# An attention and MLP kernel: dummy matmuls in the front's gaps, measured TensorE durations in the build-time order, and two value tiles loaded earlier

## The chip, the core and the metric

The kernel runs on one core of one Trainium2 chip. The metric is the device time of one execution in microseconds (us). It is compared between kernels run in alternation on the same chip. "Same" means within 2%.

The readings are of the hardware profiler's trace. In its lines PE is the TensorE matmul, PEld the weight load, DVE VectorE, ACT ScalarE, POOL GpSimd and SP SyncE. Ends of matmuls are modelled there (one of 512 columns is given 379 ns, though the next starts 216 ns after it), so a PE that is busy all the time is not necessarily at its peak.

## The reference, cut to what matters

```python
# B, H, S, Nb, D = 8, 8, 576, 16, 64; d_model 512, d_ff 2048, 4608 tokens
k_all = np.concatenate([beacon_k, k], axis=2)
v_all = np.concatenate([beacon_v, v], axis=2)
scores = 1/sqrt(D) * q @ k_all.transpose(...)        # causal on the 576 tokens
a = softmax(scores)
x = (a @ v_all) in the shape [B*S, H*D]
h = x @ w_in
out = (max(h, 0) ** 2) @ w_out
```

A batch has four pairs of heads. The MLP works in nine chunks of 512 tokens. Its first stage multiplies by w_in, its second by w_out. Chunk 0 is made of tokens of batch 0 alone, so it can't start before batch 0's attention.

## The kernel before

The kernel has no loops in its program. At build time it makes a list of operations, each with an engine, an estimated duration, a priority and dependencies, and plays them through an event simulation of its own. What comes out is a fixed order of instructions for each engine. On the chip TensorE works through its instructions in that order and stands where an input isn't there. So the estimated durations are never executed; they only decide who stands before whom.

```python
class Order:
    def run(self):
        ...
            for e in engines:
                if free[e] > now + 1e-9:
                    continue
                best = ...            # the ready op of least prio, whose buffers are free
                if best is None:
                    best = fallback
                if best is None:
                    continue          # this engine idles, in the order's own time
                ...
                end = now + dur
                free[e] = end
                issued.append((op, e, now))
                ...
                # users on PE see it `late` us later than other engines do
                heapq.heappush(events, (seen + op.late, seq, "done_pe", op))
        ...
        for op, e, _ in issued:
            op.insts = op.emit(e)
```

Two of the operations, and the order of the first loads on the GpSimd queue (t0, t1 make a mask; p1k is k of pair 1 of batch 0; v0 the first 128 rows of batch 0's v; w0 a quarter of w_in):

```python
qk = add(f"qk{p}.{n}.{i}", "PE", 0.24 + cols / 2400.0, emit_qk, ...)
tp = add(f"tp{b}.{part}.{pr}{xs}", "PE", 0.1 + (0.1 if b == 0 else 0.075) * ns * len(xs), emit_tp, ...)

RANK = [(0, 0), (0, 1), (1, 0), (1, 1), (2, 0), (3, 0), (2, 1), (3, 1)]   # (pair, phase) of batch 0
SOFT = "t0 p1k p1q t1 p2k p2q p3k p3q v0 v1 v2 v3 v4 w0 w1 w2 w3".split()
```

Behind these loads come batch 1's k and q, batch 1's v, and w_out in quarters. The loads of the queue are issued one after another: in the timeline of the kernel before k and q of pair 1 at 2.39 and 3.15 us, of pair 2 at 4.36 and 5.05, of pair 3 at 5.67 and 6.29.

The softmax here doesn't subtract the row's maximum and nothing guards it: scores larger than these inputs give would overflow.

## Time and profile before

| | before |
|---|---|
| time, median of 3 executions | 344.12 us (343.36 to 344.19) |
| TensorE busy | 332.1 of 342.1 us |
| TensorE waiting, in all | 5.8 us, of which 4.3 at the very start |
| first matmul; first matmul with w_in | 4.31 us; 23.99 us |
| DMA share of the 16 engines from 5 to 35 us | 1.10 to 1.30 |

The table of waits of the kernel before, for TensorE; the columns are who waited for whom, us in total, times, longest:

```profile
PE ps L462 <- DVE qk_area L307: 4.9, 2, 4.3
PE strip L609 <- DMA kT<-qk_area: 0.4, 1, 0.4
PE ps L661 <- DVE vb L307: 0.3, 1, 0.3
PE ps L792 <- DVE qT L307: 0.2, 1, 0.2
```

After its first matmul TensorE waits for 1.5 us in all. But the same work is slow in the front. From the timeline of the kernel before (start us, us, engine, line, operation, operands, count): 12 transposes of batch 0 and 24 of batch 1, then 24 attention-value matmuls before and after 22 us.

```profile
8.14 0.69 PE L465 MATMUL ps<-ident,qk_area 96*64 96x96 bf16 x12
30.07 0.70 PE L465 MATMUL ps<-ident,qk_area 96*64 96x96 bf16 x24
...
18.44 1.50 PE L661 MATMUL ps<-vb,pt 128*128 128x65 bf16 x24
24.40 0.89 PE L661 MATMUL ps<-vb,pt 128*128 128x65 bf16 x24
```

Twenty-four transposes at 30 us take what 12 take at 8 us, and the same 24 matmuls shrink from 1.50 to 0.89 us (the last 0.06 to 0.15 us of each overlap the group behind it, since ends are modelled). In the chain of work the 24 matmuls take 1.44 us at 18.51 and 0.73 us at 24.57: I read that as TensorE at half clock, then at full clock. The page's clock row hides it:

```profile
PE   4999999999999999999999999999999999999995
PEclk9999999999999999999999999999999999999999
```

The trace's own record of the granted clock begins with the grant of full clock at 22.5 us, counted from the first instruction. What lies before that first record is shown as full (1.00 from 5 to 20 us, where the durations are doubled). From its first matmul to that grant TensorE was busy for 17.0 of 18.2 us. Below, the clock's "release" is the time from which the record gives full clock.

### The profile page before, as it was taken

The numbers are of one execution on the slowest core, as the hardware profiler recorded it, in microseconds if no ns is written. First come the engines' busy times: TensorE is split into PE (matmuls) and PEld (weight loads), VectorE is DVE, ScalarE is ACT, GpSimd is POOL, SyncE is SP. The second block draws the span as 40 slices with busy tenths as digits, with TensorE's granted clock in tenths as the row PEclk, the third lists the DMA queues.
The fourth block names the chain that finished last, engine by engine and source line by source line (L and its number), as shares of the span: only waits on it lengthen the run. The fifth ranks groups of instructions, "written<-read, shape, count | busy, mean of one in ns | idle before, by whom it ended". The sixth has DMA issues, their size and how long they took to land.

```text
span 342.1 us, 7180 instructions
## 1 busy us (share of the span) xinstructions
PE 332.1 (97%) x2886; PEld 176.4 (52%) x2886; DVE 169.4 (50%) x371; ACT 191.9 (56%) x287; POOL 92.5 (27%) x144
## 2 busy tenths in 40 slices
PE   4999999999999999999999999999999999999995
PEld 2578775444544544445458845444444544444442
DVE  6878975147437863277436643664246502301300
ACT  4776864387766753675347744675557226515611
POOL 9774803324415605041521053014000000000000
PEclk9999999999999999999999999999999999999999
DMA  8999979999999999699989997977210131011002
GB/s 147 210 207 218 206 124 215 209 241 210 193 192 251 245 187 200 145 219 212 208 136 235 158 216 145 229 159 134 86 63 2 24 107 63 0 61 64 0 31 92
DMA packets 143663, 51.68 MB, mean 151 GB/s; under 512 B 130670, under 2 KB 138382, under 8 KB 143630
## 3 DMA queue, kind: packets, MB, share of 16 engines
q1 hardware_dynamic: 135231, 42.25, 62.1%
q0 software_dynamic: 7904, 8.69, 14.8%
q8 instruction: 22, 0.36, 0.5%
q10 hardware_dynamic: 495, 0.30, 0.3%
q14 instruction: 11, 0.09, 0.1%
HBM read 37.22 MB, written 9.44 MB: 136 GB/s over the span
## 4 chain that ended last, share of the span: by engine, by line
PE 85%; DMA 8%; POOL 3%; DVE 2%; ACT 0%; issue 0%; SPq 0%; POOLq 0%; ACTq 0%
PE ps L792 34%; PE ps L827 34%; PE ps L661 8%; PE strip L609 7%; DMA stg<-in_v_dram 3%; DMA kT<-qk_area 2%; DMA stg<-in_q_dram 2%; DMA stg<-in_k_dram 1%; POOL qk_area L430 1%; PE ps L729 1%; POOL qk_area L307 1%; DVE qT L307 1%; DVE g L817 0%; PE ps L465 0%; POOL tri L291 0%
## 5 line engine op out<-in xcount | busy, mean ns | idle before, releaser
L827 PE MATMUL ps<-w_out,g 128*128 128x512 bf16 x576 | 133.8, 379 | 0.0
L792 PE MATMUL ps<-xT,w_in 128*128 128x512 bf16 (+3 forms) x704 | 133.4, 341 | 0.2 <-DVE qT L307 0.2
L624 ACT ACTIVATE pt<-strip 128x832 bf16<-128x832 f32 (+4 forms) x128 | 104.3, 863 | 39.9 <-PE strip L609 39.7
L792 PEld LDWEIGHTS <-w_in 128*128 128x128 bf16 x704 | 65.7, 98 | 56.4 <-issue 4.3
L808 ACT ACTIVATE g<-ps 128x512 bf16<-128x512 f32 (+2 forms) x119 | 67.0, 563 | 41.6 <-PE ps L792 40.9
L827 PEld LDWEIGHTS <-g 128*128 128x128 bf16 x576 | 52.7, 98 | 60.9 <-issue 3.2
L817 DVE TENSOR_TENSOR g<-g 128x1024 bf16<-128x1024 bf16 (+2 forms) x80 | 52.5, 659 | 61.8 <-ACT g L808 59.5
L307 POOL CAST qk_area<-stg 128x512 bf16<-128x512 f32 (+2 forms) x60 | 40.3, 679 | 73.5 <-DMA stg<-in_k_dram 58.8
L305 ACT COPY osb<-ps 128x512 f32<-128x512 f32 x28 | 16.4, 585 | 57.4 <-PE ps L827 51.3
L661 PEld LDWEIGHTS <-pt 128*128 128x128 bf16 (+1 forms) x960 | 37.8, 100 | 14.8 <-issue 3.5
L307 POOL CAST vb<-stg 128x512 bf16<-128x512 f32 (+1 forms) x39 | 26.1, 678 | 62.7 <-DMA stg<-in_v_dram 44.3
L661 PE MATMUL ps<-vb,pt 128*128 128x65 bf16 (+1 forms) x960 | 41.5, 197 | 0.3 <-DVE vb L307 0.3
L609 PE MATMUL strip<-qT,kT 64*128 64x80 bf16 (+6 forms) x400 | 37.3, 292 | 0.4 <-DMA kT<-qk_area 0.4
L681 DVE TENSOR_TENSOR xn<-ps,rcp 128x320 bf16<-128x320 f32 (+2 forms) x64 | 31.5, 492 | 2.3
L635 DVE TENSOR_TENSOR pt<-pt,tri 128x1024 bf16<-128x1024 bf16 (+1 forms) x36 | 23.7, 658 | 15.8 <-ACT pt L624 15.8
L810 DVE TENSOR_SCALAR g<-ps 128x512 bf16<-128x512 f32 (+2 forms) x41 | 24.4, 603 | 14.0 <-PE ps L792 13.5
L679 DVE RECIPROCAL rcp<-ps 128x5 f32<-128x5 f32 (+2 forms) x64 | 12.2, 191 | 34.9 <-PE ps L661 34.7
L609 PEld LDWEIGHTS <-kT 64*128 64x128 bf16 x400 | 12.4, 96 | 17.6 <-issue 12.6
L307 DVE COPY osb<-ps 128x512 f32<-128x512 f32 x8 | 5.5, 692 | 19.1 <-PE ps L827 19.0
L638 DVE TENSOR_TENSOR pt<-pt,tri 80x160 bf16<-80x160 bf16 x32 | 10.3, 320 | 0.0
L352 POOL DMA_DIRECT2D stg<-in_v_dram x10 | 8.5, 850 | 5.0 <-DMA w_in<-in_moe_w_in_dram 3.6
L307 DVE COPY kT<-ps 128x576 bf16<-128x576 bf16 (+3 forms) x11 | 6.5, 594 | 1.9 <-PE ps L465 1.0
(38 smaller groups left out, 64.6 us busy)
## 6 DMA issues: line engine op xcount, KB each, us to landing
out_dram<-osb SPq DMA_DIRECT2D x17, 512.0 KB, 3.9
stg<-in_q_dram SPq DMA_DIRECT2D x24, 256.0 KB, 5.5
stg<-in_k_dram SPq DMA_DIRECT2D x18, 256.0 KB, 5.1
stg<-in_v_dram SPq DMA_DIRECT2D x18, 256.0 KB, 4.6
w_in<-in_moe_w_in_dram POOLq DMA_DIRECT2D x4, 512.0 KB, 8.9
w_out<-in_moe_w_out_dram POOLq DMA_DIRECT2D x4, 512.0 KB, 11.3
stg<-in_v_dram POOLq DMA_DIRECT2D x6, 256.0 KB, 8.3
stg<-in_k_dram SPq DMA_DIRECT2D x6, 224.0 KB, 4.7
```

The costliest lines, as they stand in the source:

```text
L305: nc.scalar.copy(dst, src)
L307: eng[e].tensor_copy(dst, src)
L609: nc.tensor.matmul(st[:, hj, at:at + t1 - t0], kT[b % 2][hp, pr, 128 * c:128 * c + 128], qT[b % 2][hp, pr, t0:t1], start=True, stop=True,)
L624: nc.scalar.activation(pt[take_pt.held[2]][:, :, off:off + width], st[:, :, 0:width], AF.Exp, bias=0.0, scale=scale)
L635: nc.vector.tensor_tensor(out=d, in0=d, in1=tri[:, m0:m0 + m, :][:, None].to_broadcast([128, 2, m, 128]), op=ALU.min)
L661: nc.tensor.matmul(a[:, at + (t - tl[0]) * (D + 1):at + (t - tl[0] + 1) * (D + 1)], P[0:rr, hj, o:o + 128], vb[b % 2][0:rr, c, 2 * pr + hj ...
L681: nc.vector.tensor_tensor(out=xn[b % 2].rearrange("p t (h d) -> p h t d", d=D)[:, h0:h0 + nh, tl[0]:tl[0] + nt], in0=a[:, :, :, 0:D], in1= ...
L792: nc.tensor.matmul(h[:, lo - spans[0][0]:hi - spans[0][0]], w_in_sb[:, mc, ft * 128:(ft + 1) * 128], xT[:, mc, lo % RING:lo % RING + hi - lo],
L808: nc.scalar.activation(dst, h, AF.Relu, bias=0.0, scale=1.0)
L810: nc.vector.tensor_scalar(out=dst, in0=h, scalar1=0.0, scalar2=None, op0=ALU.max)
L817: nc.vector.tensor_tensor(out=d, in0=d, in1=d, op=ALU.mult)
L827: nc.tensor.matmul(o, G[:, fc, ts * 128:(ts + 1) * 128], w_out_sb[:, fc, :], start=(fc == 0), stop=(fc == NFT - 1))
```

## The change

Its intent: get TensorE's clock up early with dummy matmuls, keep it up by putting dummies wherever the order expects TensorE to idle until 22 us, correct the order's TensorE durations to those measured, load v0 and v1 ahead of batch 0's last pair, and hold back the TensorE users of some loads in the order.

```diff
+    FILL_UNTIL = 22.0
 ...
                     if best is None:
+                        if e == "PE" and 0.3 < now < self.FILL_UNTIL and self.pools["ps"]:
+                            cols = 128 if now < 4.0 else 256
+                            free[e] = now + 0.107
+                            issued.append((Op("fill", "PE", 0.107, lambda e, cols=cols, bank=self.pools["ps"][0]: self.fill(bank, cols)), e, now))
 ...
+    def emit_fill(bank, cols):
+        nc.tensor.matmul(ps[bank][:, 0:cols], g[1][:, 0, 0:128], g[1][:, 0, 0:cols], start=True, stop=True)
+    nc.vector.memset(g[1][:, 0, 0:256], 0.0)
 ... (cast of v: batch 0's users on TensorE 1 us later; first q and k casts 0.3, pair loads 0.5)
-                    tp = add(..., "PE", 0.1 + (0.1 if b == 0 else 0.075) * ns * len(xs), emit_tp,
+                    tp = add(..., "PE", 0.05 + (0.055 if b == 0 else 0.047) * ns * len(xs), emit_tp,
-            qk = add(f"qk{p}.{n}.{i}", "PE", 0.24 + cols / 2400.0, emit_qk,
+            qk = add(f"qk{p}.{n}.{i}", "PE", 0.2 + cols / 2400.0, emit_qk,
 ... (three more durations of this kind)
-    RANK = [(0, 0), (0, 1), (1, 0), (1, 1), (2, 0), (3, 0), (2, 1), (3, 1)]
+    RANK = [(0, 0), (0, 1), (1, 0), (2, 0), (1, 1), (3, 0), (2, 1), (3, 1)]
-    SOFT = "t0 p1k p1q t1 p2k p2q p3k p3q v0 v1 v2 v3 v4 w0 w1 w2 w3".split()
+    SOFT = "t0 p1k p1q t1 p2k p2q v0 v1 p3k p3q v2 v3 v4 w0 w1 w2 w3".split()
```

## The prediction

> **What bounds the kernel now.** From about 25 us on TensorE does: the table of busy time by stretch has it busy 10.00 of 10 us in nearly every stretch from 40 to 335 us, and the table of waits gives it 0.7 us of waiting there at most (0.4 us at 98 us, for the kT transpose DMA). So useful TensorE work moved earlier shortens the run, while ready work lasts. The page shows idle time only at the front: until 4.31 us, 0.58 us at 5.9, 0.34 us at 14.8.

> **What the change does.** (1) Dummy 128-column matmuls from about 1 us (estimate: 25 to 35, 107 ns each) and 256-column ones in the order's gaps until 22. I expect the full clock at 5 to 8 us, seen in halved durations. The 17 us of half-clock front are some 8.5 us of work at full clock. Cost: tenths of a us where a dummy precedes ready work. (2) v0 and v1 are issued before pair 3's k and q: about 1.3 us earlier (two issues of 0.63), landing before 14.1 us; that removes the v wait. Pair 3 lands later, but nine exps of 0.86 us precede it in the new ranking. (3) Shorter model durations reorder the program; total work stays.

> **How much survives.** ScalarE: batch 0 has 16 exps of 0.86 us, 13.8 us, now 7.1 to about 25 us with gaps; could end near 21. VectorE is busy 9.2 of 10 us at 30 to 40. The DMA engines are saturated (share over 1.1) from 5 to 35 us, so w_in's quarters still land at about 20.4, 22.9, 25.4 and 28 us (from waits on them), and the last first-stage matmuls of chunk 0 can't end before about 30; w_out lands at 44 to 49 us, and second-stage matmuls now begin at 47.7. So by 34 us the new kernel can be ahead by about 40 matmuls of 272 columns at 113 ns, 4.5 us; of it some is lost to a thinner stock before w_out lands and to VectorE. Estimate: 4.3 us saved, carried to the end because the late stretches are TensorE-bound with MLP work in stock.

> **Prediction:** 339.8 us, range 336.8 to 342.8; faster by over 2%: 0.14, within 2%: 0.83, slower by over 2%: 0.03.

> **What would show it.** Right: 96-column transposes near 27 ns each from about 8 us; last exp of batch 0 ending at about 21 us; first w_in matmul at about 21 instead of 24.0 us, the last 272-column one 4 us earlier; no new waits over 1 us after 50 us. Wrong: durations still doubled at 15 us; TensorE waiting for w_in, w_out or batch 1's k and q between 22 and 50 us by as much as was gained; the 98 us wait for kT grown to several us.

> **What would make it wrong.** The dummies don't release the clock, or it falls back; the reordering starves TensorE later; or w_in and w_out arrive earlier (then 335 to 337 us).

A front of 17 us taken for 8.5 us of work, less what the loads and VectorE hold back, a lead of 4.5 us by 34 us, of which 4.3 us saved; 344.1 less 4.3 is 339.8 us. The sum takes the full clock at 5 to 8 us for granted; the kernel before, released at 22.5 us, doesn't show that, and only the changed kernel's 5.5 us bears it out.

## The result, and the profile after

The changed kernel took 343.43 us, median of 6 executions (342.86 to 344.13), against 343.83 us for the kernel before in the same rounds. A ratio in this document is the mean time of one kernel's fast runs over that of the other's of the same rounds, so it is not quite the ratio of the medians. Here it is 0.9989, with a 95% interval of 0.9972 to 1.0006. A second measurement (e12 below) gave 0.9976 (0.9957 to 0.9995). So the change saves about 0.4 us by the first, whose interval includes no gain at all, and 0.8 us by the second; the predicted 4.3 us are not there.

The clock did what was hoped for. The changed kernel's record grants the full clock at 5.5 us and keeps it until 340.0 us, 1.2 us before the last instruction. In the timeline of the changed kernel the transposes and the attention-value matmuls of batch 0 have the short durations:

```profile
5.25 1.89 PE L285 MATMUL ps<-g 128*128 128x256 bf16 x15
6.98 0.46 PE L475 MATMUL ps<-ident,qk_area 112*128 112x112 bf16 x6
...
10.28 0.45 PE L478 MATMUL ps<-ident,qk_area 96*64 96x96 bf16 x12
...
18.96 0.90 PE L674 MATMUL ps<-vb,pt 128*128 128x65 bf16 x24
```

Line 285 is the dummies. In the page's table of groups of the changed kernel (name, shapes, count, busy us, mean ns, then idle time before) they are a large item:

```profile
L285 PE MATMUL ps<-g 128*128 128x256 bf16 (+1 forms) x83 | 11.3, 291 | 1.1 <-DVE warm L292 1.1
```

All waits of TensorE in the changed kernel are these two:

```profile
PE ps L285 <- DVE warm L292: 1.1, 1, 1.1
PE ps L805 <- DVE g L823: 0.2, 1, 0.2
```

To see where a gain comes and goes I count the useful work done by a given time: each matmul that isn't a dummy counts for the median distance from start to start that its shape has in the undisturbed part of the trace before (216 ns for one of 512 columns). "Lead" is how much more of it a kernel has done than the kernel before at the same time.

| at us | 10 | 14 | 20 | 24 | 28 | 34 | 44 | 336 |
|---|---|---|---|---|---|---|---|---|
| lead of the changed kernel, us | -0.4 | -0.9 | 0.2 | 1.2 | 1.3 | 1.2 | 0.8 | 1.1 |

So by 20 us the changed kernel, at full clock for 14.5 us, has done no more than the kernel before at half clock. Nearly all of the 1.3 us that it then leads by comes between 20 and 26 us, where the kernel before still ran at half clock until 22.5, and the changed one had one dummy left. From there on the lead is carried to the end, less a few tenths. (The profiled execution of the changed kernel is the fastest of its six, 342.86 us, so its lead of 1.1 us is more than the mean gain of 0.4 us.)

Where did the clock's gain go? The kernel before spends 18.9 us on TensorE work between its first matmul and its first w_in matmul in the chain of work (24.16 less 4.31, less 0.92 of waits). The changed kernel spends 18.6 us from 4.72 to 23.33; of these, by the pieces of the same chain, 6.8 us are dummies and 11.8 us are work. The clock saved 7.1 us of work and the dummies put 6.8 us in its place. (The two stretches hold nearly the same work, not exactly the same.) This is a sum along the chain, and it doesn't say what TensorE would have done without the dummies: whether it would have worked ahead or stood and waited. e2, e9 and e11 below tell that, stretch by stretch.

The loads came where expected: w_in's quarters landed at 20.1, 22.6, 25.2 and 27.7 us before, and at 19.5, 22.7, 25.2 and 28.4 us after. v1 landed at 13.2 us in place of 14.1.

### The profile page after: what moved, and what is told of

It is laid out like the page before. It is cut to its first block, busy times and chain, and to the rows that moved or that the text cites. A ratio compares the mean times of both kernels' runs of the same rounds, so it can differ in the third digit from the quotient of the medians.

```text
span 341.2 us, 7350 instructions
## 1 busy us (share of the span) xinstructions
PE 335.9 (98%) x2969; PEld 180.2 (53%) x2969; DVE 172.6 (51%) x374; ACT 189.3 (55%) x284; POOL 94.5 (28%) x145
## 3 DMA queue, kind: packets, MB, share of 16 engines
q0 software_dynamic: 7904, 8.69, 14.9%
## 4 chain that ended last, share of the span: by engine, by line
PE 97%; DVE 2%; ACT 0%; issue 0%; DVEq 0%; ACTq 0%
PE ps L840 37%; PE ps L805 36%; PE ps L674 9%; PE strip L622 9%; PE ps L285 3%; PE ps L478 2%; PE ps L742 1%; DVE g L830 1%; DVE g L823 0%; DVE pt L648 0%; DVE qT L320 0%; PE ps L475 0%; ACT osb L318 0%; PE ps L423 0%; DVE g L291 0%
## 5 line engine op out<-in xcount | busy, mean ns | idle before, releaser
L320 POOL CAST vb<-stg 128x512 bf16<-128x512 f32 (+1 forms) x40 | 28.0, 709 | 68.4 <-DMA stg<-in_v_dram 38.7
L318 ACT COPY osb<-ps 128x512 f32<-128x512 f32 x24 | 14.0, 585 | 53.2 <-PE ps L840 51.8
L674 PEld LDWEIGHTS <-pt 128*128 128x128 bf16 (+1 forms) x960 | 36.1, 98 | 14.1 <-issue 3.4
L674 PE MATMUL ps<-vb,pt 128*128 128x65 bf16 (+1 forms) x960 | 39.7, 194 | 0.0
L622 PE MATMUL strip<-qT,kT 64*128 64x80 bf16 (+6 forms) x400 | 35.2, 277 | 0.0
L823 DVE TENSOR_SCALAR g<-ps 128x512 bf16<-128x512 f32 (+2 forms) x41 | 24.7, 611 | 13.6 <-PE ps L805 12.8
L648 DVE TENSOR_TENSOR pt<-pt,tri 128x1024 bf16<-128x1024 bf16 (+1 forms) x36 | 24.3, 676 | 11.8 <-ACT pt L637 11.7
L622 PEld LDWEIGHTS <-kT 64*128 64x128 bf16 x400 | 11.9, 94 | 17.9 <-issue 14.4
L320 DVE COPY osb<-ps 128x512 f32<-128x512 f32 x12 | 8.3, 692 | 16.8 <-PE ps L840 12.6
L285 PE MATMUL ps<-g 128*128 128x256 bf16 (+1 forms) x83 | 11.3, 291 | 1.1 <-DVE warm L292 1.1
L651 DVE TENSOR_TENSOR pt<-pt,tri 80x160 bf16<-80x160 bf16 x32 | 10.7, 334 | 0.0
```

Of the source, the lines that this page charges most:

```text
L285: nc.tensor.matmul(ps[bank][:, 0:cols], g[1][:, 0, 0:128], g[1][:, 0, 0:cols], start=True, stop=True)
L320: eng[e].tensor_copy(dst, src)
L622: nc.tensor.matmul(st[:, hj, at:at + t1 - t0], kT[b % 2][hp, pr, 128 * c:128 * c + 128], qT[b % 2][hp, pr, t0:t1], start=True, stop=True,)
L648: nc.vector.tensor_tensor(out=d, in0=d, in1=tri[:, m0:m0 + m, :][:, None].to_broadcast([128, 2, m, 128]), op=ALU.min)
L674: nc.tensor.matmul(a[:, at + (t - tl[0]) * (D + 1):at + (t - tl[0] + 1) * (D + 1)], P[0:rr, hj, o:o + 128], vb[b % 2][0:rr, c, 2 * pr + hj ...
L823: nc.vector.tensor_scalar(out=dst, in0=h, scalar1=0.0, scalar2=None, op0=ALU.max)
```

## The experiments

Two questions had to be told apart. Was the time of the dummies free, because TensorE would have waited for something else all the same (ScalarE's exps or loads), or do the dummies hold up work that is ready? And if TensorE gets ahead, does the lead last?

All ratios are to the kernel before of the same rounds. e1 to e4 ran on one chip, e5 to e16 in three groups on another, e17 and e18 on a third. Some traces of the second chip lack about 40 of the 1280 w_in and w_out matmul records, one or two of them ahead of 46 us; leads taken from them are given up to 46 us and can be 0.1 to 0.4 us too small.

| run | what | ratio (95%) | median us | full clock in the profiled run | first w_in matmul |
|---|---|---|---|---|---|
| before | | 1 | 343.83 | from 22.5 us | 23.99 |
| changed | | 0.9989 (0.9972 to 1.0006) | 343.43 | from 5.5 | 23.16 |
| e12 | changed, again | 0.9976 (0.9957 to 0.9995) | 343.07 | from 5.0 | 23.07 |
| e1 | no dummies emitted | 0.9986 (0.9973 to 0.9999) | 343.46 | from 23.2 | 24.78 |
| e2 | first 32 dummies only | 0.9999 (0.9977 to 1.0021) | 344.28 | from 17.1 | 22.81 |
| e3 | before + dummies | 1.0049 (1.0015 to 1.0083) | 345.27 | 5.9 to 16.2, from 23.0 | 27.48 |
| e4 | old order of loads and pairs | 0.9976 (0.9963 to 0.9989) | 343.00 | from 5.4 | 23.84 |
| e5 | changed, ScalarE cut | 0.9996 (0.9971 to 1.0021) | 343.06 | from 5.6 | 23.24 |
| e6 | before, ScalarE cut | 1.0008 (0.9987 to 1.0029) | 343.60 | from 21.7 | 23.91 |
| e7 | no dummies, ScalarE cut | 1.0017 (0.9995 to 1.0039) | 344.03 | from 17.4 | 23.24 |
| e8 | 21 dummies left out | 1.0004 (0.9984 to 1.0025) | 343.62 | from 14.0 | 24.50 |
| e9 | first 47 dummies only | 0.9998 (0.9972 to 1.0025) | 343.49 | 5.4 to 15.6, from 22.5 | 24.14 |
| e10 | e9, ScalarE cut | 0.9997 (0.9972 to 1.0022) | 343.64 | 4.3 to 14.5, from 17.9 | 23.32 |
| e11 | later dummies half as long | 0.9975 (0.9955 to 0.9996) | 343.25 | from 4.9 | 22.00 |
| e13 | e11, batch 1's users later | 0.9980 (0.9959 to 1.0001) | 343.23 | from 5.9 | 22.14 |
| e14 | e13, all dummies 128 columns | 0.9976 (0.9957 to 0.9994) | 343.04 | from 5.6 | 21.75 |
| e15 | e13, ScalarE cut | 0.9968 (0.9949 to 0.9986) | 342.59 | from 6.4 | 22.53 |
| e16 | changed, batch 1's users later | 0.9992 (0.9967 to 1.0016) | 343.53 | from 6.5 | 23.67 |
| e17 | e14, w_out's users later | 0.9955 (0.9939 to 0.9972) | 342.32 | 5.3 to 15.6, from 19.0 | 24.10 |
| e18 | e14, w_out before batch 1's v | 0.9938 (0.9926 to 0.9949) | 341.36 | 4.6 to 11.5, from 14.9 | 22.95 |

### e1: the same order, no dummies

```diff
-lambda e, cols=cols, bank=self.pools["ps"][0]: self.fill(bank, cols)
+lambda e, cols=cols, bank=self.pools["ps"][0]: None
```

> The changed kernel in the same order, but no dummy matmul is emitted, so the front runs at half clock again. Theory A (the dummies release the clock but stand in the queue before ready work, and the two cancel): the full clock comes at 20 us or later, the first score matmul moves from 7.4 us back to about 6.6, and the time is within 0.7 us of the changed kernel (343.4 us) either way. Theory B (full clock in the front is worth several us and something later eats it): 2 to 5 us slower than the changed kernel, because the reordering then stands alone.

Its ratio is 0.9986, the changed kernel's 0.9989. The clock came at 23.2 us. Full clock with the dummies and half clock without them give the same time. So the 83 dummies are worth nothing in sum, and the small gain doesn't need them. That fits theory A; it fits theory C of e2 as well, in which the front waits for ScalarE and loads whatever TensorE's clock is. Theory B, a gain of several us eaten later, is out.

### e2: only the dummies ahead of the first transposes

```diff
+ self.fill(bank, cols) if cols == 128 else None
```

> The changed kernel in the same order with the 32 dummies before the first transpose alone; the 51 later ones are not emitted. Theory A: the clock is released at about 5.5 us as before and holds, the second transposes start near 6 us instead of 7.0, the exps start about 1 us earlier, and the kernel gains 0.7 to 1.5 us over the changed one (about 342.3). Theory C (the front waits for ScalarE and for loads whatever TensorE does): within 0.4 us of the changed kernel. If the clock falls back to half in the gaps, that shows as doubled durations at 10 to 20 us and says what the later dummies are for.

The executions took 342.39, 342.61 and four times 344.2 to 344.5 us. The second transposes started at 5.89 us and not at 6.98, after a true wait of 0.57 us, and the first exp at 7.09 us and not 7.75. So the 15 dummies that stand between the first and the second transposes in the changed kernel held ready work up by 1.1 us:

```profile
5.89 0.74 PE L475 MATMUL ps<-ident,qk_area 112*128 112x112 bf16 x6 [0.57 <-DVE qk_area L320]
```

But 3.6 us of dense dummies did not release the clock: in the profiled execution, the one of 342.39 us, it came at 17.1 us. So this run could not settle what a full clock without later dummies gives. I didn't foresee that.

### e3: the kernel before with the dummies alone

The edit is the diff's part for the dummies and nothing else.

> The kernel before with the dummies alone: old TensorE durations in the model, old order of loads and pairs. The clock should be released at about 5.5 us. Theory A: no gain, 343.0 to 344.5 us. Theory B: the dummies bring the whole gain of the clock: 340 us or less, and the rest of the change gives it back.

It is slower than before, by 0.5%. The clock fell back at 16.2 us, and TensorE waited for v (0.9 and 0.8 us). That old durations and the old order leave longer gaps there is a guess. The first w_in matmul came at 27.48 us, 3.5 us later than before. The loss goes with a lost clock: each execution has a mean granted clock on record, and the two with 0.998 took 343.69 and 344.24 us, the four with 0.983 to 0.993 took 344.69 to 348.28. So the dummies bring nothing here, and the slow executions are those that lost the clock.

### e4: the old order of loads and pairs

```diff
-    RANK = [(0, 0), (0, 1), (1, 0), (2, 0), (1, 1), (3, 0), (2, 1), (3, 1)]
+    RANK = [(0, 0), (0, 1), (1, 0), (1, 1), (2, 0), (3, 0), (2, 1), (3, 1)]
-    SOFT = "t0 p1k p1q t1 p2k p2q v0 v1 p3k p3q v2 v3 v4 w0 w1 w2 w3".split()
+    SOFT = "t0 p1k p1q t1 p2k p2q p3k p3q v0 v1 v2 v3 v4 w0 w1 w2 w3".split()
```

> The changed kernel with the old order of loads and the old rank of the pairs (v0 and v1 after pair 3's k and q). If the new order of loads matters in itself, this is 0.5 to 1.5 us slower than the changed kernel; if pair 3's late landing (14.9 instead of 11.7 us) costs as much as the earlier v (13.2 instead of 14.1 us) brings, it is within 0.4 us of it.

0.9976, which is no worse than the changed kernel (0.9989 and 0.9976). The earlier v brings nothing measurable: pair 3's q landed at 11.5 us here and at 14.9 in the changed kernel, which may be what pays for v1's landing earlier; no wait in either trace shows it.

### e5, e6, e7: less work for ScalarE

In the changed kernel ScalarE runs exps almost without a pause from 9.3 to 23 us. I took that for the limit of the front (theory C). To test it, two of the four exps of each of batch 0's pairs are cut short. TensorE's instructions stay the same in number and order, and the attention-value matmuls read columns that are written.

```diff
+                    w = {1024: 128, 1536: 8}.get(off, width) if b == 0 else width
-                    nc.scalar.activation(pt[take_pt.held[2]][:, :, off:off + width], st[:, :, 0:width],
+                    nc.scalar.activation(pt[take_pt.held[2]][:, :, off:off + w], st[:, :, 0:w],
...
                             o = ph.off[c, t]
+                            if b == 0 and o > 1024:
+                                o -= 1024 if o >= 1536 else 512
```

e5 is the changed kernel with it, e6 the kernel before, e7 the changed kernel without dummies.

> A wrong result on purpose: the changed kernel, but two of the four exps of each of batch 0's pairs process 128 and 8 columns per head in place of 464 and 416; the attention-value matmuls read other, written columns. TensorE's instructions and order are unchanged; ScalarE has about 4.8 us less work before 23 us. Theory C (ScalarE, busy 98% from 9.3 to 23 us, sets the end of batch 0's attention): the last exp ends 2 us or more earlier and the run is 1.5 to 3 us faster than the changed kernel. Theory L (loads set it: pair 3's q lands at 14.9, w_in at 19.5 to 28.4 us): less than 0.7 us faster.

> The same cut of ScalarE's work in the kernel before, whose front runs at half clock until 22 us. If the half clock binds as soon as ScalarE no longer does, this gains under half of what the cut brings in the changed kernel: at most 1 us against before. If the clock doesn't matter at all in the front, it gains as much as the changed kernel does with the cut.

> The same cut in the changed kernel's order with no dummy emitted (half clock in the front). Against the run of the changed kernel with the cut this tells what the full clock is worth when ScalarE is out of the way: 1 to 2 us slower than it if the clock binds then, within 0.5 us if it still doesn't.

None gained (0.9996, 1.0008 and 1.0017). ScalarE in the changed kernel, and then in e5, from the timelines:

```profile
9.28 5.00 ACT L637 ACTIVATE pt<-strip 128x832 bf16<-128x832 f32 x6 [0.75 <-PE strip L622]
14.50 3.49 ACT L637 ACTIVATE pt<-strip 128x928 bf16<-128x928 f32 x4 [0.23 <-PE strip L622]
```

```profile
14.58 0.38 ACT L638 ACTIVATE pt<-strip 128x256 bf16<-128x256 f32 x1 [0.23 <-PE strip L622]
15.24 0.18 ACT L638 ACTIVATE pt<-strip 128x16 bf16<-128x16 f32 x1 [0.28 <-PE strip L622]
16.37 1.14 ACT L638 ACTIVATE pt<-strip 128x832 bf16<-128x832 f32 x2 [0.95 <-PE strip L622]
```

ScalarE now has pauses, and each ends with TensorE (the releaser in brackets). TensorE did not go any faster: its lead over the kernel before is the same as the changed kernel's to about 0.1 us at every point up to 40 us, and the first w_in matmul is at 23.24 us in place of 23.16. For the changed kernel as it stands theory C is wrong: TensorE waits for nobody there, because it is kept busy by its own queue. This says what the dummies are: the build-time order put one wherever it expected TensorE to wait, and all 83 are executed in e5 too, where ScalarE's part of the wait isn't needed. They turn an expected wait, which costs nothing if the input is early, into one that is always paid (1.1 us ahead of the second transposes, by e2). But e5 doesn't say that the waits were imaginary: as long as the dummies stand in for a wait for ScalarE, cutting ScalarE's work can't show. For that the dummies have to go, as in e9 and e10.

e6 and e7 say that ScalarE doesn't set the time at half clock either (e7's clock came at 17.4 us). In both it is mostly TensorE's half-clock work, plus a few waits (0.7 us for v in e6; 0.6 us for pair loads and 1.2 us for ScalarE in e7).

### e8, e9, e10: fewer dummies

```diff
 e8: skip=4.0 <= now < 8.0   ->  self.fill(bank, cols) if not skip else None
 e9: early=now < 6.0         ->  self.fill(bank, cols) if early else None
 e10: e9, with ScalarE's work cut as in e5
```

> The changed kernel in the same order; only the 21 dummies that the order placed between 4 and 8 us of its own time are not emitted: the 15 ahead of the second transposes and the 6 after them. Theory A in part: the first exp starts at about 7.1 instead of 7.75 us and the second at 8.2 instead of 9.3, the full clock comes at 5.5 us and is kept by the later dummies, and the run is 0.4 to 1.0 us faster than the changed kernel. If the clock falls back or comes late, as with the 32 dummies alone, no gain.

> The changed kernel in the same order with its first 47 dummies (those up to 6 us of the order's own time, which run until about 7.2 us), and none of the 36 later ones. The cut of ScalarE's work changed nothing in the changed kernel, so theory A now reads: from 5 us on TensorE never waits there, because dummies stand in its queue for as long as the order expected it to wait. Then, if the clock comes at 5.5 us and holds, TensorE reaches the first w_in matmul 0.3 to 1.0 us earlier than in the changed kernel (23.2 us), waits for ScalarE show up, and the run gains 0.3 to 1.0 us. If the clock falls back between 9 and 17 us, the later dummies were what held it, and there is no gain or a loss of up to 1 us.

> A wrong result on purpose: as e9_first47 with the cut of ScalarE's work. If dummies are what hid ScalarE's cut in the changed kernel, and the clock holds, this gains 1 to 2.5 us over e9_first47 (first w_in matmul at 21 to 22 us). If loads limit the front, it is within 0.5 us of e9_first47. If the clock falls back, within 0.7 us of it too: then half clock paces the front, as in the kernel before.

None gained in time (1.0004, 0.9998 and 0.9997), and none had the full clock all through the front. In e8 the release came at 14.0 us. In e9 and e10 it came at 5.4 and 4.3 us but fell back at 15.6 and 14.5. e9's timeline shows the fall and the next rise:

```profile
14.63 0.45 PE L478 MATMUL ps<-ident,qk_area 96*64 96x96 bf16 x12 [0.62 <-DMA qk_area<-in_q_dram]
...
18.36 1.50 PE L674 MATMUL ps<-vb,pt 128*128 128x65 bf16 x24
...
23.26 0.89 PE L674 MATMUL ps<-vb,pt 128*128 128x65 bf16 x24
```

So the later dummies are perhaps more than padding: both profiled executions without them (e9, e10) lost the clock, and three of the thirteen with them (e3, e17, e18). What makes it fall is not shown: TensorE's longest wait between release and fall was 0.6 us in e9 and 1.0 us in e18. Nor is it shown what brings the release, only when it came: at 4.3 to 6.5 us in the profiled runs of all fourteen kernels with dummies right behind the first transposes, at 17.1 and 14.0 us in e2 and e8, which have only the 32 ahead of these, and at 17.4 to 23.2 us in the four without dummies (before, e1, e6, e7).

Until the fall, e9 and e10 show what no other run does: the front at full clock and without dummies. TensorE's waits in e9 and then in e10, up to 50 us (the lines of 0.4 us and more; of e10 without the wait for the first dummies):

```profile
PE strip L622 <- ACT pt L637: 1.2, 3, 0.4
PE ps L285 <- DVE warm L292: 1.1, 1, 1.1
PE ps L478 <- DMA qk_area<-in_q_dram: 0.6, 1, 0.6
PE strip L622 <- DVE qT L320: 0.4, 1, 0.4
```

```profile
PE ps L478 <- DMA qk_area<-in_k_dram: 1.7, 1, 1.7
PE strip L622 <- ACT pt L638: 1.4, 3, 0.7
PE strip L622 <- DVE qT L320: 0.4, 1, 0.4
```

Between 7.3 and 15 us the changed kernel has 24 dummies, 3.25 us of its chain. e9 has none of them, and yet reaches the first group of 12 attention-value matmuls only 0.43 us earlier, at 15.00 in place of 15.43 us: it stands 2.2 us for ScalarE (1.2), VectorE (0.4) and pair 3's q (0.6) instead, ScalarE running eight exps without a pause from 8.81 to 14.97 us. So in this stretch most of the dummies stand where TensorE would have waited. With ScalarE's work cut as well, e10 gets to the last score matmuls ahead of pair 3's transposes at 12.26 us (12.75 in e9, but e10's earlier clock had put it 0.4 us ahead at the start), and then stands 1.7 us for pair 3's k, which lands at 14.33. So at full clock this stretch is limited by ScalarE and, last of all, by the landing of pair 3's k and q, at 13.2 and 14.6 us in e9. With the old order of loads, e4, they land at 10.7 and 11.5: it is the change itself that put them behind v0 and v1. So theories C and L of e5 hold for this stretch, once the dummies are out of the way. This rests on one profiled execution of each, and nobody ran e9 with the old order of loads. What the front would do at full clock without dummies after 15 us no run shows.

### e11: dummies of half the length

The order counts 107 ns for a dummy. At full clock the chip took 109 ns for one of 256 columns in the changed kernel (median from start to start), so 128 columns should need about half (an estimate; the 15 early ones of e18 below took 1.01 us, so at most 67 ns each, the last one's modelled end included). The order stays the same, and TensorE gets slack to catch up with.

```diff
-                            cols = 128 if now < 4.0 else 256
+                            cols = 128 if now < 4.0 or now > 6.0 else 256
```

> The changed kernel with all its dummies, but those after 6 us of the order's time have 128 columns and not 256, so that each should take about 56 ns in place of 107 while the order still counts 107. Theory A: the clock holds, TensorE gets up to 1.8 us of slack (36 dummies), the first w_in matmul comes 0.3 to 0.8 us earlier, and the run is 0.3 to 0.8 us faster than the changed kernel. No change if ScalarE or the loads pace the front.

Theory A is confirmed in part: the clock held, and the first w_in matmul came at 22.00 us, 1.07 us earlier than in e12, the changed kernel in the same rounds (e11, then e12):

```profile
22.00 0.57 PE L805 MATMUL ps<-xT,w_in 128*128 128x240 bf16 x4
23.07 0.57 PE L805 MATMUL ps<-xT,w_in 128*128 128x240 bf16 x4
```

The 36 halved dummies take 1.8 us less of TensorE's time, from start to start (3.0 in place of 4.8 us); 0.5 us of that went into a wait for pair 3's k at 13.6 us, and the rest into waits too short for the table. The lead at 24 to 28 us is 2.3 to 2.5 us in place of 1.3 to 1.4. But the time is the same as e12's (0.9975 and 0.9976). The lead is down to 1.35 us at 34 us. The table of waits of e11 names what took most of it; 0.8 us of the first line is a single wait at 29.35 us (the other 0.5 us is pair 3's k, above):

```profile
PE ps L478 <- DMA qk_area<-in_k_dram: 1.2, 2, 0.8
PE ps L285 <- DVE warm L292: 1.1, 1, 1.1
PE ps L805 <- DVE g L823: 0.2, 1, 0.2
```

Batch 1's k landed at 29.31 us, as it does at 29.2 in the kernel before and in the changed one. TensorE came to its transposes earlier and stood.

### e12: the changed kernel again

> The changed kernel unchanged, on the same chip and in the same rounds as the three others, to compare them with: 0.997 to 1.001 of the kernel before.

0.9976 (0.9957 to 0.9995), used above for comparison with e9 to e11.

### e13, e14, e15, e16: batch 1's users later in the queue

```diff
 e13: e11, and for the loads of batch 1's k and q
-  after = [add_part_load(b, 0, prs, x, prio + n, after, [], 1.5, 1.5)]
+  after = [add_part_load(b, 0, prs, x, prio + n, after, [], 1.5, 3.2)]
 e14: e13, and
-                            cols = 128 if now < 4.0 or now > 6.0 else 256
+                            cols = 128
 e15: e13, with ScalarE's work cut as in e5
 e16: the changed kernel with the first of these edits only
```

> As e11_half, and the order counts batch 1's q and k as ready for TensorE 1.7 us later (3.2 in place of 1.5), so three more groups of w_in matmuls stand before the first transposes. If the landing of batch 1's k is what took back the lead: no wait for it over 0.3 us, a lead of 2 us or more over the kernel before at 34 us, and 1.5 to 2.5 us saved against it (342 us or less, ratio 0.993 to 0.996). If the lead is lost all the same by 50 us (VectorE busy 9 of 10 us there, w_out landing at 42 to 49 us): ratio 0.997 to 0.998, as e11_half.

> As e13_half_late, and the 15 dummies before the second transposes have 128 columns too, so that those start about 0.5 us earlier (6.5 instead of 7.0 us). If every 0.1 us of dummies in front of ready work counts: another 0.3 to 0.6 us faster than e13_half_late. If the clock is released later for it (8 us or more), no gain.

> A wrong result on purpose: e13_half_late with the cut of ScalarE's work in batch 0. With dummies of half the length TensorE has 1.9 us of slack; if ScalarE used it up, this is 0.5 to 1.5 us faster than e13_half_late; if TensorE is still paced by its own stream, within 0.4 us.

> The changed kernel with full dummies and only the later place of batch 1's users. The lead there is 1.3 us at 28 us and the wait for batch 1's k 0 to 0.3 us, so there is little to take: within 0.6 us of the changed kernel (ratio 0.997 to 0.999).

In e13 nothing is waited for at batch 1's k and q (the 0.3 us that its table gives to a q is pair 3 of batch 0, at 14.4 us), and a lead of 2.0 to 2.5 us stood from 24 to 46 us. In e14 it was 2.4 to 2.9 us. So batch 1's loads were what took e11's lead at 30 us. Yet the times hardly moved (0.9980 and 0.9976). The waits of e14 name the next station:

```profile
PE ps L285 <- DVE warm L292: 1.1, 1, 1.1
PE ps L840 <- DMA w_out<-in_moe_w_out_dram: 1.1, 2, 0.8
PE ps L478 <- DMA qk_area<-in_k_dram: 0.7, 2, 0.3
```

The waits for w_out are at 46 to 49 us; the lead falls from 2.6 us at 46 to about 1.2 us at 50 us. The last line is k of batch 0's pairs 2 and 3, at 9.4 and 13.3 us: the front again waits for loads as soon as its dummies shrink. In the kernel before the last quarter of w_out lands at 49.48 us.

e15 against e13 (0.9968 and 0.9980, intervals that overlap widely) shows no effect of ScalarE that could be told from noise, even with slack on TensorE, and its first w_in matmul is later, at 22.53 us. e16 gained nothing, as expected, and had a wait of 0.7 us for w_out too.

### e17, e18: w_out

```diff
 e17: e14, and for the four loads of w_out:  dma=2.6  ->  dma=2.6, late=2.0
 e18: e14, and the order of the queue:
-  behind=[v_loads[1][4]] if i == 0 else [w_ops["out", i - 1]]
+  behind=[strided[1, 0, HP - 1, "q"]] if i == 0 else [w_ops["out", i - 1]]
-    v_loads[1][0].behind[:] = [strided[1, 0, HP - 1, "q"]]
+    v_loads[1][0].behind[:] = [w_ops["out", 3]]
```

> As e14_all128_late, and the order counts w_out as ready for TensorE 2 us later, so that the users of its last quarter stand about 1.6 us later in the queue. If w_out's landing is what took the lead at 46 to 50 us: waits for it 0.4 us or less in place of 1.1, a lead of about 2 us at 55 us, and about 0.8 us faster than e14: ratio 0.994 to 0.996, 342 us. If something else takes it (VectorE, ScalarE, the next loads): within 0.3 us of e14, ratio 0.997 to 0.998.

> As e14_all128_late, with w_out loaded before batch 1's v, which lands about 5 to 10 us later; second-stage matmuls take the place of attention-value ones between 44 and 54 us. No wait for w_out at 46 to 50 us. If nothing else binds there, ratio 0.994 to 0.996; if batch 1's v or batch 2's loads now come too late, TensorE waits for them by 1 us or more and the run is 0.998 to 1.005.

e17 reached 0.9955, e18 0.9938 (0.9926 to 0.9949), a median of 341.36 us; both results are right. The waits of TensorE in e18, over the whole run:

```profile
PE ps L285 <- DVE warm L292: 1.1, 1, 1.1
PE ps L478 <- DMA qk_area<-in_k_dram: 1.0, 1, 1.0
```

w_out now lands at 36.3 to 44.3 us and batch 1's v at 46.1 to 50.7; nothing waits for either. e18's trace is complete. Its lead is 1.5 us at 28 us, 1.9 at 50 and 1.9 at 336 us: what is left of the lead at 50 us arrives at the end. In this profiled execution the clock fell back from 11.5 to 14.9 us, after a wait of 1.0 us for pair 2's k, so its lead at 28 us is under e14's 2.7. It was its slowest execution, 341.90 us; by the mean granted clock one more lost it so (0.993, 341.81 us), and the three without a loss (0.998 and 0.999) took 341.10 to 341.36 us. e18's interval lies below those of the changed kernel and of the kernel before. It is the best version found, 2.2 us or 0.6% faster than the kernel before, still well inside "same". e18 and e14 ran on different chips and differ by 0.4%; e17 and e18 have an unlike order of loads, and I have not tried e18's order of loads without the shorter dummies. So how much of e18's gain is owed to the loads alone stays open.

The profiled execution of e17 was its slowest, 343.79 us against 341.25 for its fastest; in it the clock was at half from 15.6 to 19.0 us and pair 3's k was waited for by 1.4 us. It is no picture of e17's typical run.

## Why the prediction was wrong

It said 339.8 us, within 336.8 to 342.8; it is 343.4. Point by point:

- **Half clock in the front: right.** The durations (1.44 us at 18.51, 0.73 us at 24.57 for 24 matmuls) and the clock's record agree (full clock from 22.5 us).
- **Dummies release the clock at 5 to 8 us: right** for the changed kernel (5.5 us, 5.0 in e12), though no trace had shown it beforehand, and with the first 32 dummies alone the release came at 17.1 us (e2).
- **"The 17 us of half-clock front are some 8.5 us of work at full clock. Cost: tenths of a us where a dummy precedes ready work": this is the step that failed.** The clock did shorten the work, by 7.1 us. But the dummies in the path, after the first transposes alone, took 6.8 us of TensorE's time, not tenths. Part of that holds ready work up, by more than tenths: 1.1 us ahead of the second transposes (e2), and 1.07 us of the 1.8 us by which e11 shortens the later ones. The other part stands in for waits that a faster TensorE really has: at full clock without dummies (e9) it stood 2.2 us for ScalarE, VectorE and pair 3's q between 7.3 and 15 us, and was 0.43 us ahead where 3.25 us of dummies had gone. So the step failed twice: the dummies' cost was mis-sized, and 8.5 us of work was taken for the length of the front, which at that pace waits for exps and loads. How the 6.8 us divide after 15 us stays open.
- **"Ahead by about 40 matmuls, 4.5 us, by 34 us": the lead there was 1.2 us**, and 0.2 us at 20 us. (The matmuls of 272 columns that it counted at 113 ns measure 116.) The first w_in matmul came at 23.16 us, not at about 21.
- **Last exp at about 21 us: wrong.** It ended at 23.0 us. Cutting 4.8 us of ScalarE's work changed nothing while the dummies stand (e5) or at half clock (e6); at full clock without dummies TensorE does wait for it, 1.2 us up to 15 us (e9).
- **Earlier v: right in time (13.2 instead of 14.1 us), worth nothing (e4).** Pair 3, which it put behind, lands at 14.9 in place of 11.7 us, and its q is one of e9's waits.
- **Landing of w_in and w_out: right** within 1 us, but for w_out's first quarter (42.1 us, not 44). I named w_out and a thinner stock of work as limits; e13, e14 and e18 show them, but only for versions that get that far ahead. In the changed kernel they can have taken a few tenths at most, since its lead is 1.3 us at 28 and 1.1 us at the end.
- **No new waits over 1 us after 50 us: right.**
- **"Carried to the end because the late stretches are TensorE-bound": right** for what there was: 1.2 us at 34 and 1.1 at 336 us.

So the change exchanges half clock for padding, and half clock had cost less than it seemed, because at full clock the front waits (2.2 us between 7.3 and 15 us in e9). The gain that the clock offers is claimed in several places one after the other: by ScalarE and the loads of batch 0's pairs up to 15 us, by the dummies, without which both profiled runs lost the clock (e9, e10), by batch 1's k at 29 us, and by w_out at 42 to 49.5 us.

## What to carry to other kernels

In this kernel a dummy in the static queue was not idle time made useful: it was a wait that no longer got shorter when the input came early (e2: 1.1 us of ready work held up). Make dummies shorter than the gaps that they stand for (e11: first w_in matmul 1.07 us earlier), and check by taking work from the engine that you believe to be the limit; if nothing moves, as in e5, the busy engine may be pacing itself. Then take the padding out and repeat the check, since padding of the length of a wait hides the wait (e9: 2.2 us). When a front is relieved, look for the next load whose landing doesn't move with it (batch 1's k at 29.2 to 29.3 us in the kernel before, the changed one and e11), and change who stands before whom in the DMA queue (e18: the last of w_out at 44.3 us in place of 49.48), before counting the gain.
